# GpSimd's share of a depthwise convolution: the tap as a tensor operand, and five of six sums made by accumulating DMAs

## The chip, the cores and the metric

The kernel runs on one core of a Trainium2 chip, as one launch. The metric is device time in microseconds (us), the median of several executions. Beside it there is a profile: one execution recorded by the hardware profiler, with every instruction's start and duration on the five engines: TensorE (PE in the profile; its weight loads are PEld), VectorE (DVE), ScalarE (ACT), GpSimd (POOL) and SyncE (SP), and with the DMA engines' work. A "q" behind an engine's name is its queue of DMA issues and semaphore waits.

## The reference

A causal depthwise convolution along the sequence (7 taps, softmax-normalised, one set for each of 8 heads of 24 channels), followed by a gated feed-forward network whose last two matrices are multiplied with nothing between them.

```python
# x: (8, 3904, 192), weight: (8, 7)
w = exp(weight - max) / (sum + 1e-09)              # over the 7 taps
x_pad = concatenate([zeros(B, 6, D), x], axis=1)   # each of the 8 sequences begins with zeros
out = einsum('hk,bskhg->bshg', w, x_unf)           # out[s] = sum over k of w[h,k] * x_pad[s+k]
...
a = x @ w1            # x: (31232, 192), w1, w2: (192, 1024)
b = x @ w2
h = a * b @ w3        # w3: (1024, 1024)
return h @ w_out      # w_out: (1024, 192)
```

Inputs and output are fp32; the kernel multiplies in bf16.

## The kernel before, in words

**Rounds and phases.** The 31232 tokens are taken as two streams of 15616 (`NS = 2`), each in rounds of `CH = 512` tokens: 31 rounds, both streams together in a round. `w3 @ w_out` is formed once at the start (`W_sb`), so that a round has two parts on TensorE. In `first_product(R)` (L599) eight tiles of 128 columns of `x @ w1` and `x @ w2` go to PSUM (`pa`, `pb`); ScalarE copies `pa` to `asb` (L606) and VectorE multiplies `asb` by `pb` into `abT` (L608). In `second_product(R, r)` (L624) `abT @ W_sb` is formed for one stream; ScalarE copies the result to `osb` (L629) and SP's queue stores it (L638). Three rounds make a phase: three first products, then the six second products of the three rounds, then the next phase. `abT` has three buffers, one for each round of a phase.

**The convolution, in three ways.** The first products need the convolved `x` transposed: channels on partitions (64 of each stream), tokens along the free dimension, three groups `k` of 64 channels. Most rounds get it from TensorE: GpSimd loads windows of `x` into `xb` (L158), a small matmul with banded weights convolves them (`conv`, L331, at the places between second products that the table `places` lists), the result goes to DRAM as `rows` and comes back through DMA transposes into a ring, `xT` (L429). Where a sequence begins inside a window, GpSimd clears rows of `xb` (`clear`, L863) before `conv` reads them. The rounds of the phases named in `SIDE` get theirs another way, as "side tasks": GpSimd casts `x` to bf16 in DRAM (`rows_c`, L483), a DMA transpose on SP's queue brings a piece with 16 tokens of halo to SBUF as `raw` (L492), and a sum over seven shifted products gives a part of `side`: ScalarE makes the first product (`side_first`), VectorE the other six as one instruction each (`side_sums`, L515). VectorE's sums run during the second products, from a plan that is worked out beforehand.

**GpSimd's half tasks.** Seven halves of such tasks (512 tokens, channel group 2) are GpSimd's: `BY_POOL`, one in each phase from the third phase of the kernel on. SP's queue brings the raw piece by one transpose (L536, `pool_transpose`) at the end of a phase's first products. In the next phase `pool_sums` gives seven jobs: the first (d = 1) writes tap times shifted raw to `acc` in fp32; the next five (d = 2 to 6) write the product to `tmp` (L542) and add `tmp` to `acc` (L562); the last (d = 0) writes a product to `tmp` and adds it to `acc` into `side` in bf16 (L557). `tmp` is one tile of 128 x 512 fp32.

**What sets GpSimd's order.** GpSimd runs its list in order. Each phase from the second on has eight pacing points inside its first products (`points`). At each, a tiny copy from the `abT` tile just written (`pace`, L879) makes GpSimd wait until VectorE has come so far; then come the `xb` loads or `rows_c` casts that are due at this point, issued from GpSimd's own DMA queue, and then one job of the half task. At the seventh point of a phase that has convolutions, `clear` stands ahead of the cast and the job. A DMA issue that must wait for something waits in the engine's queue, with everything behind it.

Of the kernel before, what the change touches and what calls it, by code (L numbers as in the profile page):

```python
# [8 lines left out]
FP32 = mybir.dt.float32  # L9
BF16 = mybir.dt.bfloat16  # L10
AX = mybir.AxisListType
ALU = mybir.AluOpType
# [4 lines left out]
def kernel(  # L17
# [10 lines left out]
    nc = tc.nc  # L28

    B, S, D = x.shape  # L30
    H, K = weight.shape
# [7 lines left out]
    CH = 512  # L39
# [30 lines left out]
    t0 = (LAG + 3) * CH  # L70
# [19 lines left out]
    const = ctx.enter_context(tc.tile_pool(name="const", bufs=1))  # L90
# [90 lines left out]
    for r in range(NS):  # L181
# [13 lines left out]
        out=diag, in_=diag, pattern=[[-1, 128 + 8]], compare_op=ALU.is_equal,  # L195
# [13 lines left out]
    for i in range(4):  # L209
        d = diag[i * C:i * C + C, i * C + 2 * i:i * C + 2 * i + C]  # L210
        nc.vector.tensor_copy(
            out=cmask[i * C:i * C + C],
            in_=bass.AP(tensor=d.tensor, offset=d.offset, ap=[d.ap[0], [1, 2], [1, C]]))
# [45 lines left out]
    for i in range(3):  # L259
# [3 lines left out]
        out=share[:, :, 0:K], in0=taps.unsqueeze(1).to_broadcast([H, H, K]), scalar=total,  # L263
        in1=diag[0:H, 0:H].unsqueeze(2).to_broadcast([H, H, K]), op0=ALU.mult, op1=ALU.mult)
    spread = banks("spread")
    for i in range(4):
# [6 lines left out]
        out=wsb, in_=spread[:, 0, 0:2 * H].rearrange("p (h k) -> p h k", h=H)  # L273
# [5 lines left out]
        out=cprod.rearrange("p h k (s two) -> p h k s two", two=2),  # L279
        in0=cmask.rearrange("p k (s two) -> p k s two", two=2).unsqueeze(1)  # L280
            .to_broadcast([128, H, 2, C // 2, 2]),
        in1=wsb.unsqueeze(3).to_broadcast([128, H, 2, C // 2, 2]),
        op=ALU.mult)
# [6 lines left out]
    for k in range(2):  # L290
# [5 lines left out]
                          in_=bps[:, 0, 0:C * H].rearrange("p (h s) -> p h s", s=C))  # L296
# [137 lines left out]
    wC = const.tile([128, NP, K], FP32)  # L434
# [85 lines left out]
        size = (t1 - t0) / (2 * CH)  # L520
        return [(size, job(d, d == 0)) for d in list(range(2, K)) + [0]]

    pool_raw, pool_acc, pool_tmp = [], [], const.tile([128, CH], FP32, name="tmp")

    def pool_tiles():
        t = stage.tile([128, 3 * CH + HALO], BF16, tag="wo", bufs=1, name="acc")
# [3 lines left out]
    def pool_half(p, k, half):  # L530
        lo = half_of(p, half)[0]
        return p, k, lo, [z for z in range(0, TS, S) if lo <= z < lo + CH]
# [5 lines left out]
    def pool_sums(p, k, half):  # L538
        _, _, t0, starts = pool_half(p, k, half)

        def product(out, d):
            nc.gpsimd.tensor_scalar(  # L542
                out=out, in0=pool_raw[0][:, HALO - d:HALO - d + CH],
                scalar1=wC[:, k, K - 1 - d:K - d], scalar2=None, op0=ALU.mult)

        def job(d):
            def run():
                acc, tmp = pool_acc[0], pool_tmp
                if d == 1:
                    product(acc, 1)  # L550
                    for z in starts:
                        nc.gpsimd.memset(acc[:, z - t0:z - t0 + 1], 0.0)
                    return
                product(tmp, d)
                if d == 0:
                    o = half * CH
                    nc.gpsimd.tensor_tensor(out=side_of[p][:, k, o:o + CH], in0=acc, in1=tmp,  # L557
                                            op=ALU.add)
                    return
                for lo, hi in zip([t0] + [z + d for z in starts], starts + [t0 + CH]):  # L560
                    a = acc[:, lo - t0:hi - t0]
                    nc.gpsimd.tensor_tensor(out=a, in0=a, in1=tmp[:, lo - t0:hi - t0],  # L562
                                            op=ALU.add)
            return run
        return [job(d) for d in list(range(1, K)) + [0]]

# [382 lines left out]
```

## Time and profile before

| | us |
|---|---|
| median of 3 runs (lowest, highest) | 512.19 (511.61, 513.01) |
| span of the profiled execution, first to last instruction | 509.2 |
| TensorE busy | 504.4 |
| VectorE busy | 446.6 |
| ScalarE busy | 347.4 |
| GpSimd busy | 229.3 |

The page names no other time of the profiled execution than its span; the run's time is some 3 us above it. The granted TensorE clock is 1.000 over the span. Rows of a group give line, engine, operation, output and inputs, shapes, the count, then the busy time in us, the mean duration in ns and the idle time just before. Rows of a timeline give start and duration in us, then line, engine, operation and count. Rows of DMA issues end with the size in KB and the median time in us from issue to landing. A row of waits gives the waiting engine, tile and line, what released it, then the total in us, the number of times and the longest.

### The profile page before, as it was taken

The page shows a single profiled execution, that of the slowest core. Times are in us where ns is not written, and L with a number is a line of the kernel's source. Part 1 is how long each engine was busy: PE and PEld are TensorE (multiplying, and loading weights), DVE is VectorE, ACT ScalarE, POOL GpSimd, SP SyncE. Part 2 cuts the span into 40 slices and gives each one's busy share as a digit, 9 for nine tenths or more (in the row PEclk, how much of TensorE's full clock was granted, in tenths as well). Part 3 has the DMA queues.
Part 4 walks back from the last instruction along what each step waited for, and adds up shares of the span by engine and source line. Part 5 has one row for each costly group of instructions (what it writes and reads, how often), then busy time and mean ns, then how long its engine had stood idle before and what let it go on. Part 6 is the DMA issues. An engine that isn't in the chain of part 4 may idle for free.

```text
span 509.2 us, 13689 instructions
## 1 busy us (share of the span) xinstructions
PE 504.4 (99%) x5761; PEld 338.9 (67%) x5761; DVE 446.6 (88%) x403; ACT 347.4 (68%) x387; POOL 229.3 (45%) x303
## 2 busy tenths in 40 slices
PE   8999999999999999999999999999999999999997
PEld 4546865595569557855875596569557855965597
DVE  7898769999999799899989999999899999999930
ACT  6786667836778776477667767763776477457752
POOL 9966101333990597079519902970573067100000
PEclk9999999999999999999999999999999999999999
DMA  9999979999966999973889337986501500230025
GB/s 135 161 158 179 171 145 181 149 158 190 166 60 160 142 158 126 237 79 23 65 220 95 25 105 123 194 111 158 102 0 44 156 2 0 84 106 1 1 64 156
DMA packets 156825, 58.45 MB, mean 115 GB/s; under 512 B 112607, under 2 KB 156763, under 8 KB 156763
## 3 DMA queue, kind: packets, MB, share of 16 engines
q1 hardware_dynamic: 86043, 40.62, 38.0%
q0 software_dynamic: 70560, 16.85, 37.2%
q8 instruction: 45, 0.74, 0.6%
q14 instruction: 17, 0.14, 0.1%
q10 hardware_dynamic: 160, 0.10, 0.1%
HBM read 33.97 MB, written 34.85 MB: 135 GB/s over the span
## 4 chain that ended last, share of the span: by engine, by line
PE 98%; DVE 1%; ACT 0%; issue 0%
PE ops L624 32%; PE pa L599 31%; PE pb L599 31%; PE cps L331 1%; PE wps L696 1%; PE warm L241 1%; PE tps L404 0%; PE ops L649 0%; PE tps L419 0%; DVE abT L608 0%; PE cps L360 0%; ACT asb L606 0%; ACT convo L340 0%; DVE xb L285 0%; DVE Aband L295 0%
## 5 line engine op out<-in xcount | busy, mean ns | idle before, releaser
L608 DVE TENSOR_TENSOR abT<-asb,pb 128x1024 bf16<-128x1024 bf16 x240 | 292.7, 1221 | 30.4 <-ACT asb L606 14.5
L606 ACT CAST asb<-pa 128x1024 bf16<-128x1024 f32 x244 | 247.0, 1012 | 64.2 <-PE pa L599 64.0
L599 PEld LDWEIGHTS <-wn 64*128 64x128 bf16 x1488 | 138.5, 94 | 79.7 <-issue 1.6
L599 PEld LDWEIGHTS <-ws 64*128 64x128 bf16 x1488 | 129.7, 94 | 70.0 <-issue 1.4
L624 PE MATMUL ops<-W_sb,abT 128*128 128x192 bf16 x1936 | 163.7, 246 | 0.0
L624 PEld LDWEIGHTS <-abT 128*128 128x128 bf16 x1936 | 158.5, 98 | 6.4 <-issue 6.4
L599 PE MATMUL pb<-xT,wn 64*128 64x512 bf16 x408 | 111.2, 376 | 0.0
L599 PE MATMUL pa<-xT,wn 64*128 64x512 bf16 x408 | 110.1, 376 | 0.1
L599 PE MATMUL pa<-xT,ws 64*128 64x512 bf16 x408 | 110.2, 376 | 0.0
L599 PE MATMUL pb<-xT,ws 64*128 64x512 bf16 x408 | 108.5, 376 | 0.0
L629 ACT COPY osb<-ops 128x768 f32<-128x768 f32 (+1 forms) x61 | 48.5, 795 | 84.7 <-PE ops L624 82.8
L879 POOL COPY pace<-abT 1x2 bf16<-1x2 bf16 x57 | 10.9, 192 | 175.2 <-DVE abT L608 175.2
L599 PE MATMUL pb<-side,wn 64*128 64x512 bf16 (+1 forms) x336 | 88.8, 368 | 0.0
L599 PE MATMUL pa<-side,wn 64*128 64x512 bf16 (+1 forms) x336 | 87.3, 369 | 0.0
L599 PE MATMUL pa<-side,ws 64*128 64x512 bf16 (+1 forms) x336 | 87.3, 369 | 0.0
L515 DVE SCALAR_TENSOR_TENSOR acc<-raw,wC,acc 128x1024 f32<-128x1024 bf16 (+2 forms) x70 | 84.8, 1212 | 2.0
L599 PE MATMUL pb<-side,ws 64*128 64x512 bf16 (+1 forms) x336 | 85.7, 368 | 0.0
L542 POOL TENSOR_SCALAR tmp<-acc,wC 128x512 f32<-128x512 bf16 x42 | 65.7, 1565 | 1.2
L562 POOL TENSOR_TENSOR acc<-acc,tmp 128x512 f32<-128x512 f32 x35 | 44.4, 1268 | 2.9
L483 POOL DMA_DIRECT2D rows_c<-in_x_dram x50 | 37.1, 745 | 4.9 <-issue 2.8
L158 POOL DMA_DIRECT2D xb<-in_x_dram x50 | 32.3, 650 | 7.5 <-DMA xb<-in_x_dram 2.1
L515 DVE SCALAR_TENSOR_TENSOR acc<-side,wC,acc 128x1024 f32<-128x1024 bf16 (+1 forms) x20 | 24.3, 1217 | 3.8 <-DMA rows<-convo 3.2
(78 smaller groups left out, 188.5 us busy)
## 6 DMA issues: line engine op xcount, KB each, us to landing
out_dram<-osb SPq DMA_DIRECT2D x54, 384.0 KB
xb<-in_x_dram POOLq DMA_DIRECT2D x16, 240.0 KB, 7.6
out_dram<-osb SPq DMA_DIRECT2D x12, 192.0 KB
rows_c<-in_x_dram POOLq DMA_DIRECT2D x16, 130.0 KB, 4.6
rows_c<-in_x_dram POOLq DMA_DIRECT2D x12, 128.0 KB, 5.7
rows<-convo SPq DMA_DIRECT2D x6, 240.0 KB
xb<-in_x_dram POOLq DMA_DIRECT2D x6, 228.0 KB, 4.5
w3b<-in_moe_w_dram POOLq DMA_DIRECT2D x4, 256.0 KB, 5.4
```

The source lines that it names most:

```text
L158: nc.gpsimd.dma_start(out=tiles[js[0]][0][group(r, e), s:s + w, :], in_=bass.AP(tensor=x.tensor, offset=(r * TS + t - PAD) * D, ap=[[D, C] ...
L241: nc.tensor.matmul(t[:, j % 2, 0:wd].rearrange("p (a c) -> p a c", c=128), zeros, zeros.unsqueeze(1).to_broadcast([128, wd // 128, 128]), ...
L483: nc.gpsimd.dma_start(out=rows_c[lo:t1, k, r * Q:r * Q + Q], in_=x_rows[r * TS + lo:r * TS + t1, k * Q:k * Q + Q])
L515: nc.vector.scalar_tensor_tensor(out=side_of[p][:, k, o:o + t1 - t0] if last else a, in0=raw[:, HALO + lo - t0 - d:HALO + hi - t0 - d], sc ...
L542: nc.gpsimd.tensor_scalar(out=out, in0=pool_raw[0][:, HALO - d:HALO - d + CH], scalar1=wC[:, k, K - 1 - d:K - d], scalar2=None, op0=ALU.mult)
L562: nc.gpsimd.tensor_tensor(out=a, in0=a, in1=tmp[:, lo - t0:hi - t0], op=ALU.add)
L599: nc.tensor.matmul(p[:, r, f * N:f * N + N], w_of(i, k, r)[rs, ft * 128:(ft + 1) * 128], operand(R, k, rs), start=(k == 0), stop=(k == NP ...
L606: nc.scalar.copy(out=asb[:, :, 0:per * N], in_=pa[:, :, 0:per * N])
L608: nc.vector.tensor_tensor(out=ab[:, f0, :, 0:N], in0=asb[:, :, 0:N], in1=pb[:, :, 0:N], op=ALU.mult)
L624: nc.tensor.matmul(ops[:, g // 2, (g % 2) * D:(g % 2) * D + D], ab[:, jt, r, g * 128:(g + 1) * 128], W_sb[:, jt, :], start=(jt == 0), stop ...
L629: nc.scalar.copy(out=osb.rearrange("p (a g) d -> p a (g d)", g=2), in_=ops[:, 0:ng // 2, 0:2 * D])
L879: P(out=pace, in_=abT_of[R][0:1, ft, 1, 0:2])
```

## The change

`tmp` becomes two tiles that alternate with the tap. The product is a `tensor_tensor` whose second operand is the tap broadcast along the free dimension (step 0) in place of a `tensor_scalar` with the tap as a scalar. The sums of d = 2 to 6 are DMAs from GpSimd's queue that add `tmp` into `acc` in SBUF, in fp32; the last sum (d = 0) stays an instruction of GpSimd. In all seven tasks none of the five sums is split by a sequence's beginning, so there are 35 such DMAs of 128 x 512. On TensorE, VectorE and ScalarE the instructions and their order are as before, and so is the order of GpSimd's list, with the new instructions in the place of the old. Each accumulating DMA waits for the one before it on `acc` and for the product in `tmp`; the product of d = 0 waits for the DMA of d = 6, which reads the same `tmp`.

```diff
-    pool_raw, pool_acc, pool_tmp = [], [], const.tile([128, CH], FP32, name="tmp")
+    pool_raw, pool_acc = [], []
+    pool_tmp = [const.tile([128, CH], FP32, name=f"tmp{v}", tag=f"tmp{v}") for v in range(2)]
...
         def product(out, d):
-            nc.gpsimd.tensor_scalar(
+            nc.gpsimd.tensor_tensor(
                 out=out, in0=pool_raw[0][:, HALO - d:HALO - d + CH],
-                scalar1=wC[:, k, K - 1 - d:K - d], scalar2=None, op0=ALU.mult)
+                in1=wC[:, k, K - 1 - d:K - d].to_broadcast([128, CH]), op=ALU.mult)
 
         def job(d):
             def run():
-                acc, tmp = pool_acc[0], pool_tmp
+                acc, tmp = pool_acc[0], pool_tmp[d % 2]
...
                 for lo, hi in zip([t0] + [z + d for z in starts], starts + [t0 + CH]):
-                    a = acc[:, lo - t0:hi - t0]
-                    nc.gpsimd.tensor_tensor(out=a, in0=a, in1=tmp[:, lo - t0:hi - t0],
-                                            op=ALU.add)
+                    nc.gpsimd.dma_start(out=acc[:, lo - t0:hi - t0],
+                                        in_=tmp[:, lo - t0:hi - t0], accum_op=ALU.add)
```

## The prediction

> **What bounds the kernel now.** I read the page's busy times first, then the chain that ended last, then who waited on TensorE.
>
> ```profile
> span 509.2 us, 13689 instructions
> PE 504.4 (99%) x5761; PEld 338.9 (67%) x5761; DVE 446.6 (88%) x403; ACT 347.4 (68%) x387; POOL 229.3 (45%) x303
> PE 98%; DVE 1%; ACT 0%; issue 0%
> PE warm L241 <- DVE zeros L180: 1.1, 1, 1.1
> PE cps L331 <- DVE Aband L295: 0.3, 1, 0.3
> PE tps L419 <- ACT convo L340: 0.2, 1, 0.2
> L542 POOL TENSOR_SCALAR tmp<-acc,wC 128x512 f32<-128x512 bf16 x42 | 65.7, 1565 | 1.2
> L562 POOL TENSOR_TENSOR acc<-acc,tmp 128x512 f32<-128x512 f32 x35 | 44.4, 1268 | 2.9
> ```
>
> TensorE is busy 504.4 of 509.2 us and carries 98% of the chain; all its waits for others add up to 1.6 us, at the start (lines four to six). GpSimd (POOL) is not on the chain, so nothing taken off it shortens the run by itself. It can only lengthen it, by being late for TensorE. So I looked for where GpSimd's results meet TensorE with the least time in between. That is the end of the first products of the phase that begins at 117 us, the first with a half task:
>
> ```profile
> 126.02 0.17 POOL L879 COPY pace<-abT 1x2 bf16<-1x2 bf16 x1
> 126.14 1.36 POOL L158 DMA_DIRECT2D xb<-in_x_dram  x2
> 127.53 1.57 POOL L542 TENSOR_SCALAR tmp<-acc,wC 128x512 f32<-128x512 bf16 x1
> 129.19 1.27 POOL L562 TENSOR_TENSOR acc<-acc,tmp 128x512 f32<-128x512 f32 x1
> 130.40 0.18 POOL L879 COPY pace<-abT 1x2 bf16<-1x2 bf16 x1
> 130.52 0.85 POOL L483 DMA_DIRECT2D rows_c<-in_x_dram  x1
> 131.41 1.57 POOL L542 TENSOR_SCALAR tmp<-acc,wC 128x512 f32<-128x512 bf16 x1
> ...
> 145.92 0.18 POOL L879 COPY pace<-abT 1x2 bf16<-1x2 bf16 x1
> 146.15 0.56 POOL L863 MEMSET xb<- 6x192 bf16 x2
> ...
> 149.06 1.27 POOL L557 TENSOR_TENSOR side<-acc,tmp 128x512 bf16<-128x512 f32 x1
> 150.28 1.17 POOL L879 COPY pace<-abT 1x2 bf16<-1x2 bf16 x1
> ```
> ```profile
> 148.20 2.81 PE L624 MATMUL ops<-W_sb,abT 128*128 128x192 bf16 x32
> 150.94 0.42 PE L331 MATMUL cps<-xb,Aband 32*32 32x240 bf16 x30
> ```
> ```profile
> L331 PEldq EVENT_SEMAPHORE  x5: 51/51/51, 5.0 to 150.3; - x5
> ```
>
> One round at a pacing point costs GpSimd 3.9 us (130.40 to 134.3: pace copy, cast, product, sum). The two memsets (L863) clear rows of `xb` that the convolution at 150.94 reads; the last row shows TensorE's semaphore for it, at 150.3. The memsets end at 146.15 + 0.56 = 146.71, so this meeting has 150.94 - 146.71 = 4.2 us to spare, the least of any. TensorE is in order: a memset later than that stops it.
>
> **The change part by part.** *The product* (49 times L542) takes its tap as a second tensor. No row has this form; bounds are 1.27 us (L562, two tensors) and 1.57 us (as now). By form the first is nearer: I take 1.27. It saves 49 x 0.3 = 15 us of GpSimd, worth nothing on the chain.
>
> *The sums.* 35 x 1.27 = 44.4 us of GpSimd go; 35 DMA issues come, at about 0.60 us by the next-named row (35 x 0.60 = 21 us), each of 256 KB, added into `acc`.
>
> ```profile
> L677 POOL DMA_DIRECT2D w3b<-in_moe_w_dram x12 | 7.1, 599 | 1.3 <-DMA xb<-in_x_dram 1.3
> ```
>
> On GpSimd's own time the change is a gain. But *each accumulating DMA waits until the one before it on `acc` has landed*, and the wait stands in GpSimd's queue: behind it stand the next pace copy, the next cast or `xb` load, the next product and, in this phase, the memsets. Sum d issued at T is followed by pace, cast and product (0.17 + 0.85 + 1.27, some 3 us with the issue), then GpSimd stands until T + L, L being the time from issue to landing. The chain's step is max(3.0, L), against 3.9 now. No row shows an accumulating DMA; the nearest are
>
> ```profile
> rows_c<-in_x_dram POOLq DMA_DIRECT2D x4, 130.0 KB, 4.0
> xb<-in_x_dram POOLq DMA_DIRECT2D x2, 216.0 KB, 7.9
> rows_c<-in_x_dram POOLq DMA_DIRECT2D x2, 64.0 KB, 2.6
> ```
> ```profile
> xb<-in_x_dram POOLq DMA_DIRECT2D x6, 228.0 KB, 4.5
> w3b<-in_moe_w_dram POOLq DMA_DIRECT2D x4, 256.0 KB, 5.4
> DMA  9999979999966999973889337986501500230025
> ```
> ```profile
> DMA  6447999999699999999900699209900694001670
> ```
>
> the first three and the last (slices of 0.875 us) from the DMA view of 120 to 155 us alone. Below 2.6 there is no reason to go, above 7.9 (two loads behind each other on saturated engines) neither. `w3b` reads 512 KB in fp32 and writes 256 KB, the same bytes as an accumulate (two fp32 operands read, one written): 5.4, in a burst. A sum has one 130 KB cast for company in each step instead of a burst; its row is 4.0. I take L = 5.0, nearer to the row with the same bytes. Cheaper than that, by the first: 4.0.
>
> By the Trainium skill, DMA: Bandwidth & Descriptors, section Anatomy of one DMA — SWDGE (gpsimd) path, a DMA from this queue costs about 2.0 us plus its bytes at 436 GB/s, as an estimate 2.6 us here, or 3.2 with the read doubled. By it no wait would be left and the time would be the present one, while the trace's loaded rows (4.0 to 7.9) lie above it; it stands beside the second rival below.
>
> *The sum for this phase.* The first product ends at 127.53 + 1.27, so the first accumulate is issued at 128.9. It lies behind two `xb` loads (126.14, 7.9 us: landing at 134.0 and, issued 0.7 later, 134.7), in a stretch where the slices read 9 until 137. For its own transfer behind them I allow the 1.4 us by which the 130 KB cast is longer than the 64 KB one (4.0 - 2.6): it lands at 136.1. The next three sums land at 136.1 + 3L = 151.1; then the sixth sum may be issued (0.6), then pace (0.17, and see below), then both memsets (0.2 + 0.56). Pace now falls beside VectorE's side sums, where it took 1.17 instead of 0.17 (150.28 above, with VectorE's row from 149.84 below): +1.0.
>
> 151.1 + 0.6 + 0.17 + 1.0 + 0.2 + 0.56 = 153.6, against 150.94: TensorE stands 2.7 us, 2.8 with its semaphore (0.05). In general the stall is 3L - 12.2, and nothing from L = 4.1 down: 4.0 us at 5.4, 11.5 at 7.9.
>
> ```profile
> 149.84 6.85 DVE L515 SCALAR_TENSOR_TENSOR acc<-raw,wC,acc 128x1024 f32<-128x1024 bf16 x5
> ...
> 157.93 6.56 DVE L515 SCALAR_TENSOR_TENSOR acc<-raw,wC,acc 128x1024 f32<-128x1024 bf16 x5
> ...
> 167.95 5.05 DVE L608 TENSOR_TENSOR abT<-asb,pb 128x1024 bf16<-128x1024 bf16 x4 [2.14 <-ACT asb L606]
> ```
>
> *VectorE beside a late GpSimd.* The five sums that start at 149.84, beside GpSimd's last add, take 6.85 us, the same five later 6.56. GpSimd's last product and add now fall wholly among such rows; VectorE may lose up to 2 x 1.27 us. Cover: the 2.14 us for which it waits at 167.95, and TensorE's own stall; I cost it at nothing, and at up to 2 us a phase where that cover is gone. The Trainium skill, SBUF — State Buffer, section Who interferes with whom, says that a VectorE instruction with two SBUF inputs contends with a GpSimd instruction that reads SBUF, and that the later one blocks entirely; the 1.17 against 0.17 agrees.
>
> *Later half tasks.* These have no memset to meet; TensorE meets `side` itself, a phase later.
>
> ```profile
> 178.11 1.27 POOL L562 TENSOR_TENSOR acc<-acc,tmp 128x512 f32<-128x512 f32 x1
> ...
> 196.77 1.27 POOL L557 TENSOR_TENSOR side<-acc,tmp 128x512 bf16<-128x512 f32 x1
> ```
> ```profile
> 213.12 0.39 PE L599 MATMUL pa<-side,wn 64*128 64x512 bf16 x1
> ```
>
> In the second one the first sum goes out at 177.7; five landings and the last product and add give 177.7 + 5L + 2.8 = 205.5 at L = 5, for `side` at 213.1: 7.6 us to spare, gone at L = 6.5. The first, third, fifth and sixth tasks have most of a phase or more; the fourth and the seventh are as the second. So one phase pays.
>
> *SP's queue.* The transpose for the next half task (L536) waits for GpSimd's last product, six output stores behind it:
>
> ```profile
> SPq L536 <- POOL tmp L542: 35.6, 2, 20.3
> SPq L395 <- DVE convo L236: 25.7, 1, 25.7
> ```
>
> It stood up to 20.3 us already without TensorE waiting, so 5 to 9 us more cost nothing; if that cover failed, the next phase's half task would begin late by as much.
>
> *Sum.* The span 509.2 + 2.8 = 512.0; what lies around the span is 512.19 (median) - 509.2 = 3.0. Time: 515.0 us.
>
> **The rivals.**
>
> *No wait left: not slower (512.2).* If L is 4.1 or less, as the `rows_c` rows say (2.6, 4.0), the steps fit the pacing and the memsets come by 151 at the latest. For it: SBUF at both ends, and 2 KB per row where a cast moves 128-byte pieces. Against: every row above with 200 KB or more is at 4.5 or above, and the DMA engines read 9 when the first sum goes out. This is also where the Trainium skill's sum above would end.
>
> *The accumulate is dear (525 and up).* At L = 7 the first phase loses 3 x 7 - 12.2 = 8.8 us, and the second half task gives 177.7 + 35 + 2.8 = 215.5 against 213.1: 2.4 more, and the fourth about as much: some 13 us, 525. At 7.9 the first loses 11.5, the second 177.7 + 39.5 + 2.8 - 213.1 = 6.9, the fourth and the seventh up to that: about 540. For it: the `xb` row, and that an add in flight has no price here. Against: those loads stood in line for each other. It decides above L = 6.5.
>
> *Faster.* 44.4 us of sums and the products' 15 leave GpSimd, and VectorE could gain where they shared. Against: TensorE's waits are 1.6 us, none of them on GpSimd; the 0.3 us at 149.84 is the only overlap that I found. At best 511.9.
>
> **How the numbers follow.** Less than 0.3% (1.5 us) counts as no change; a measurement of this kernel can tell about that much. Forecast (L from 4.1 to 6.5, 512.5 to 520): 0.50. No wait left: 0.27. Dear: 0.19. Faster: 0.04. Of the forecast the piece under 1.5 us (L below 4.5) has 0.05, so same is 0.32, slower 0.64, faster 0.04. The predicted time is the forecast's 515.0. For 8 in 10 the range takes in the second rival from 511.7 and the dear one to L = 7.3, 530; left out are the faster case, scatter below 511.7, and the dear case's upper half. The forecast's own range is 512.5 to 520.
>
> **What would show it.** The issue-to-landing time of the new `acc<-tmp` DMAs: 5 us is right, under 4 is the second rival, over 6.5 the third. GpSimd's waits: DMA issues on L562 held by the DMA before, about 2 us each, 4 to a task. TensorE's waits: one on the memset of L863 near 151 us, of 3 us, and none elsewhere; the phases after it unchanged in length. The products: 1.27 us. The prediction is wrong if TensorE shows no wait on GpSimd, or shows waits on `side`, or if VectorE's wait of 2.14 us at a phase's start vanishes and TensorE waits there instead.

## The result, and the profile after

| | before | after |
|---|---|---|
| median (lowest to highest), us | 512.3 (511.61 to 513.01) | 515.58 (514.04 to 517.42) |
| ratio to before, 95% interval | | 1.0082 (1.0063 to 1.0101) |
| span of the profiled execution, us | 509.2 | 515.6 |

The kernel is slower. The interval, taken on 512.3, is 3.2 to 5.2 us. The four executions do not lie around one value: 514.04 and 514.43 had a granted TensorE clock of 1.000 over the span (spans 512.3 and 512.7), 516.73 and 517.42 one of 0.997 (spans 514.9 and 515.6). The profile that follows is of the one at 517.42. In every execution on record whose span was noted the time is 1.6 to 1.9 us above the span. The 3.0 us that stood around the span of before are thus some 1.8, and the other 1.2 us, as an estimate, are what the profiled execution was quicker than the median.

The page, with the engines' busy times, the chain that ended last and the waits of TensorE, answers to the first fence of the prediction; among them stand GpSimd's products and the new DMAs (median us to landing):

```profile
span 515.6 us, 13720 instructions
PE 506.7 (98%) x5761; PEld 340.3 (66%) x5761; DVE 453.4 (88%) x403; ACT 347.5 (67%) x387; POOL 199.6 (39%) x303
PE 84%; DVE 4%; issue 4%; POOL 3%; DMA 3%; SPq 1%; ACT 1%; POOLq 0%; DVEq 0%
L543 POOL TENSOR_TENSOR tmp<-acc,wC 128x512 f32<-128x512 bf16 x42 | 51.5, 1225 | 15.9 <-DMA acc<-tmp 15.8
acc<-tmp POOLq DMA_DIRECT2D x35, 256.0 KB, 3.8
PE cps L331 <- POOL xb L863: 2.5, 1, 2.5
PE pb L599 <- DVE abT L608: 1.4, 2, 0.8
```

GpSimd's busy time fell from 229.3 to 199.6 us, and the run became longer. TensorE's share of the chain fell from 98% to 84%, and DMA, GpSimd and "issue" (the wait of a DMA issue for the landing before it is booked partly as that) came into it. TensorE has waits that it did not have: one on the memsets of L863, and two small ones on VectorE's `abT`.

GpSimd's timeline of the first half task (start, duration, line, operation; idle time ahead in brackets) answers to the rows from 126.02 to 146.15 of before:

```profile
128.78 0.96 POOL L562 DMA_DIRECT2D acc<-tmp  x1 [0.31 <-POOL tmp L543]
...
138.23 0.90 POOL L562 DMA_DIRECT2D acc<-tmp  x1 [6.56 <-issue]
...
143.76 0.89 POOL L562 DMA_DIRECT2D acc<-tmp  x1 [2.70 <-issue]
...
148.56 0.90 POOL L562 DMA_DIRECT2D acc<-tmp  x1 [2.00 <-issue]
...
150.11 2.04 POOL L543 TENSOR_TENSOR tmp<-acc,wC 128x512 f32<-128x512 bf16 x1
152.56 0.90 POOL L562 DMA_DIRECT2D acc<-tmp  x1 [0.41 <-POOL tmp L543]
153.18 0.32 POOL L879 COPY pace<-abT 1x2 bf16<-1x2 bf16 x1
153.54 0.56 POOL L863 MEMSET xb<- 6x192 bf16 x2
```

From one accumulate to the next it takes 9.45, 5.53, 4.80 and 4.00 us, where one round took 3.9 before. The brackets show GpSimd standing for 6.56, 2.70 and 2.00 us ahead of a DMA. The profile names no releaser for these three; by the time to landing of the DMA before (8.9, 4.7 and 4.2 us in the DMA view of each), every one of them ended 0.6 to 0.8 us after that landing. The memsets, at 146.15 before, come at 153.54. TensorE's timeline at that place:

```profile
148.32 2.81 PE L624 MATMUL ops<-W_sb,abT 128*128 128x192 bf16 x32
151.07 0.30 PE L331 MATMUL cps<-xb,Aband 32*32 32x240 bf16 x10
153.84 0.69 PE L331 MATMUL cps<-xb,Aband 32*32 32x240 bf16 x22 [2.48 <-POOL xb L863]
154.47 4.36 PE L624 MATMUL ops<-W_sb,abT 128*128 128x192 bf16 x32
158.76 0.45 PE L331 MATMUL cps<-xb,Aband 32*32 32x240 bf16 x32
```

The wait is in the third row, 2.48 us. The rows around it are longer too: the convolution, now in two parts, takes 0.30 + 0.69 us for the 0.42 of one block, and the 32 matmuls behind it 4.36 us where such 32 take 2.81 in the first row. That is 0.57 + 1.55 us on top of the wait. The table of stretches of the same execution has the reason for the 1.55 (length, busy time of each engine with its count, granted clock, DMA share, GB/s):

```profile
152.00:156.00 4.00, 2.11 (x38) 1.74 (x38) 3.89 (x4) 1.40 (x2) 2.20 (x6) 0.94 0.98 114
156.00:160.00 4.00, 4.00 (x61) 3.31 (x60) 3.14 (x2) 1.55 (x4) 3.55 (x2) 0.64 0.96 67
160.00:164.00 4.00, 4.00 (x51) 4.00 (x50) 1.37 (x2) 3.25 (x5) 1.02 (x3) 1.00 0.28 20
```

The clock was 0.94 in the stretch with the wait, 0.64 in the next, and 1.00 after it. These are means: in stretches of half a microsecond the clock is 1.00 up to 155.5 us, 0.50 from there to 158.9, and 1.00 again. So TensorE ran at half speed for 3.4 us, and that began 1.7 us after it had resumed at 153.84. By the Trainium skill, TensorE: Matmul & The Clock Gate, Part 1, the clock halves after an idle window of about 3.4 us; the trace agrees on the half, but here it fell behind a wait of 2.5 us, so the measurement puts the point lower.

The rest lies later, ahead of two phases that begin at 314 and at 362 us, and comes through VectorE. For the first of them, VectorE's timeline, then GpSimd's, then TensorE's rows that waited:

```profile
300.01 8.11 DVE L515 SCALAR_TENSOR_TENSOR acc<-raw,wC,acc 128x1024 f32<-128x1024 bf16 x5
```
```profile
303.48 1.35 POOL L543 TENSOR_TENSOR tmp<-acc,wC 128x512 f32<-128x512 bf16 x1 [2.15 <-DMA acc<-tmp]
304.91 2.13 POOL L558 TENSOR_TENSOR side<-acc,tmp 128x512 bf16<-128x512 f32 x1
```
```profile
318.30 0.37 PE L599 MATMUL pb<-side,wn 64*128 64x512 bf16 x1 [0.85 <-DVE abT L608]
...
366.18 0.37 PE L599 MATMUL pb<-xT,wn 64*128 64x512 bf16 x1 [0.57 <-DVE abT L608]
```

Five sums that took 6.56 us before take 8.11, while GpSimd's last product and add stand among them, held back by landings. VectorE then reaches the next first products late, and TensorE waits 0.85 us for `abT`; the same again a phase later, 0.57.

Where the time went, from the lengths of TensorE's phases in the two profiles: the second products of the phase from 117 us 22.42 against 17.78 (+4.64: 2.48 wait, 0.57 for the split convolution, 1.55 for the clock), the first products from 314 us +0.97, those from 362 us +0.69, and +0.1 near the start. That is 6.4 us = 515.6 - 509.2. The two executions with clock 1.000 have spans 3.1 and 3.5 us above 509.2, less than 6.4 - 1.55; how the 3.1 to 3.5 split up there no profile shows.

### The profile page after: what moved, and what is told of

Same layout as the page of the kernel before. It is cut to its first block, busy times and chain, and to the rows that moved or that the text cites. A ratio compares the mean times of both kernels' runs of the same rounds, so it can differ in the third digit from the quotient of the medians.

```text
span 515.6 us, 13720 instructions
## 1 busy us (share of the span) xinstructions
PE 506.7 (98%) x5761; PEld 340.3 (66%) x5761; DVE 453.4 (88%) x403; ACT 347.5 (67%) x387; POOL 199.6 (39%) x303
## 4 chain that ended last, share of the span: by engine, by line
PE 84%; DVE 4%; issue 4%; POOL 3%; DMA 3%; SPq 1%; ACT 1%; POOLq 0%; DVEq 0%
PE ops L624 28%; PE pa L599 27%; PE pb L599 27%; DVE acc L515 3%; DMA acc<-tmp 1%; DVE abT L608 1%; PE cps L331 1%; SPq L492 1%; PE wps L696 1%; DMA wn<-in_moe_w_dram 1%; POOL tmp L543 1%; ACT asb L606 1%; POOL xb L158 1%; DMA acc<-rows_c 0%; PE tps L404 0%
## 5 line engine op out<-in xcount | busy, mean ns | idle before, releaser
L515 DVE SCALAR_TENSOR_TENSOR acc<-raw,wC,acc 128x1024 f32<-128x1024 bf16 (+2 forms) x70 | 90.1, 1287 | 5.4 <-ACT acc L497 3.4
L879 POOL COPY pace<-abT 1x2 bf16<-1x2 bf16 x57 | 16.4, 287 | 138.8 <-DVE abT L608 138.7
L543 POOL TENSOR_TENSOR tmp<-acc,wC 128x512 f32<-128x512 bf16 x42 | 51.5, 1225 | 15.9 <-DMA acc<-tmp 15.8
L562 POOL DMA_DIRECT2D acc<-tmp x35 | 31.6, 902 | 62.3 <-issue 32.5
L483 POOL DMA_DIRECT2D rows_c<-in_x_dram x50 | 39.3, 790 | 3.2 <-issue 3.1
L340 ACT CAST convo<-cps 128x320 bf16<-128x320 f32 (+4 forms) x42 | 25.0, 670 | 4.2 <-PE cps L331 4.2
```

What stands on the lines that cost most here:

```text
L340: f(out=convo[:, e::E, k, :, lo:lo + c] .rearrange("p w r g -> p r w g"), in_=src[:, :, :, o:o + c])
L483: nc.gpsimd.dma_start(out=rows_c[lo:t1, k, r * Q:r * Q + Q], in_=x_rows[r * TS + lo:r * TS + t1, k * Q:k * Q + Q])
L515: nc.vector.scalar_tensor_tensor(out=side_of[p][:, k, o:o + t1 - t0] if last else a, in0=raw[:, HALO + lo - t0 - d:HALO + hi - t0 - d], sc ...
L543: nc.gpsimd.tensor_tensor(out=out, in0=pool_raw[0][:, HALO - d:HALO - d + CH], in1=wC[:, k, K - 1 - d:K - d].to_broadcast([128, CH]), op=A ...
L562: nc.gpsimd.dma_start(out=acc[:, lo - t0:hi - t0], in_=tmp[:, lo - t0:hi - t0], accum_op=ALU.add)
L879: P(out=pace, in_=abT_of[R][0:1, ft, 1, 0:2])
```

## The experiments

Theory: the chain of landings holds back the memsets of L863, and TensorE's wait there, with what it brings along, is the loss. Rivals: the 35 transfers load the DMA engines for everyone; the new product disturbs VectorE; or GpSimd's lateness as such costs VectorE time, wherever it comes from. The third column counts the executions whose mean granted clock over the span was below 0.9985.

| experiment | median (range), us | executions with less clock | ratio to before (95%) |
|---|---|---|---|
| e1, memsets ahead of the chain | 515.21 (512.94 to 518.46) | 4 of 12 | 1.0075 (1.0051 to 1.0100) |
| e2, the product alone | 511.05 (510.84 to 512.18) | 0 of 11 | 0.9991 (0.9975 to 1.0006) |
| e3, DMAs in the first task alone | 514.38 (512.23 to 516.78) | 3 of 10 | 1.0054 (1.0030 to 1.0077) |
| e4, DMAs in all tasks but the first | 513.17 (512.63 to 516.20) | 3 of 12 | 1.0044 (1.0023 to 1.0065) |
| e5, two accumulators | 513.05 (511.96 to 514.27) | 0 of 7 | 1.0037 (1.0023 to 1.0050) |
| e6, kernel before, memsets held by 8 us | 516.97 (515.24 to 519.05) | 5 of 6 | 1.0113 (1.0092 to 1.0134) |
| e7, kernel before with 35 unread DMAs | 512.57 (511.96 to 515.81) | 3 of 10 | 1.0039 (1.0022 to 1.0056) |
| e8, copying DMAs | 511.65 (one execution) | | |
| e9, DMAs in the fourth and fifth task | 512.78 (511.98 to 513.89) | 0 of 8 | 1.0030 (1.0020 to 1.0040) |
| e10, as e7 with the new product | 510.95 (510.84 to 512.06) | 1 of 11 | 0.9995 (0.9986 to 1.0004) |
| e11, as e6, held by 5.8 us | 512.88 (512.45 to 513.48) | 0 of 6 | 1.0029 (1.0018 to 1.0041) |

The kernel before, on the same chips, had medians of 511.05 to 511.21.

### e1: the memsets at the fifth pacing point of that phase, in place of the seventh

```diff
         if p in places:
-            at[last - 1].insert(0, clear)
+            at[4 if p == 2 else last - 1].insert(0, clear)
```

> The changed kernel with one move: in the phase from 117 us the memsets of xb stand at the fifth pacing point instead of the seventh. Theory (late memset): TensorE's wait on L863 (2.5 us) and the lower granted clock behind it go; what is left is VectorE's lateness at the start of two later phases, up to 1.4 us: 512.3 to 514.0 us. Rival (the 9 MB that the accumulating DMAs move slow the other transfers): nothing changes, 515 to 516.

The wait on L863 is gone, as expected. The time did not follow: 515.21, above the 512.3 to 514 that was expected and within the 515 to 516 of the rival, the load (e10, below, speaks against that one). TensorE's waits and GpSimd's timeline of e1:

```profile
PE pb L599 <- DVE abT L608: 2.2, 2, 1.5
PE pa L599 <- POOL side L558: 1.5, 1, 1.5
```
```profile
177.67 0.93 POOL L562 DMA_DIRECT2D acc<-tmp  x1 [0.31 <-POOL tmp L543]
...
210.84 2.06 POOL L543 TENSOR_TENSOR tmp<-acc,wC 128x512 f32<-128x512 bf16 x1 [6.11 <-DMA acc<-tmp]
212.97 2.12 POOL L558 TENSOR_TENSOR side<-acc,tmp 128x512 bf16<-128x512 f32 x1
```

The same DMA in the profile of the change:

```profile
182.53 0.93 POOL L562 DMA_DIRECT2D acc<-tmp  x1 [0.31 <-POOL tmp L543]
```

In e1 the second half task runs up to the time when TensorE needs `side`. Its first accumulate goes out at 177.67, its last product starts at 210.84, 33.2 us later, and `side` is done at 215.09; TensorE was there at about 213.6. In the change the same stretch took 27.5 us (182.53 to 210.05), and `side` was done in time.

It is tempting to say that the change's stall in the first phase had paid for this second meeting. The two profiles speak against it. GpSimd is tied to TensorE by the pacing copies, so the stall moved both: the first accumulate goes out 4.86 us earlier in e1, and TensorE begins the phase in which it needs `side` 4.86 us earlier too (213.01 for 217.87). In both there are 35.3 us from the one to the other. What differs is how long the landings took, and why they took longer in e1's profiled execution no run shows.

TensorE's phases in e1 say where its 4.1 us of span are: the first products from 213 us are 1.71 longer than before (the wait on `side`), those from 311 us 1.67 and those from 360 us 0.82 (the waits on `abT`). So taking away the one wait that a profile shows gave back nothing that can be measured, because other meetings, with landings that differ from profile to profile, cost as much.

### e2: the product alone

```diff
-            nc.gpsimd.tensor_scalar(
+            nc.gpsimd.tensor_tensor(
                 out=out, in0=pool_raw[0][:, HALO - d:HALO - d + CH],
-                scalar1=wC[:, k, K - 1 - d:K - d], scalar2=None, op0=ALU.mult)
+                in1=wC[:, k, K - 1 - d:K - d].to_broadcast([128, CH]), op=ALU.mult)
```

> The kernel before with the product as tensor_tensor and the five sums left on GpSimd. Theory: GpSimd is ahead of its old times by some 0.4 us a step, TensorE waits for nothing: 512.2 +- 0.6 us, no change. Rival (a two-operand product contends with VectorE, or is itself dear): 513 or more, and VectorE's L515 or L608 rows longer than before.

Level with before. The page of e2 and its groups show what the form costs by itself:

```profile
PE 504.0 (99%) x5761; PEld 338.9 (67%) x5761; DVE 445.7 (88%) x403; ACT 347.4 (68%) x387; POOL 204.2 (40%) x303
L542 POOL TENSOR_TENSOR tmp<-acc,wC 128x512 f32<-128x512 bf16 x42 | 43.8, 1044 | 0.5
```

1.04 us for 1.57: 25 us less for GpSimd, which is on nobody's path. Half of the change is free of harm and of use; the loss is in the DMAs.

### e3 and e4: the DMAs in the first half task alone, and in all but the first

```diff
+                    a = acc[:, lo - t0:hi - t0]
+                    if (p, half) == (5, 0):
+                        nc.gpsimd.dma_start(out=a, in_=tmp[:, lo - t0:hi - t0],
+                                            accum_op=ALU.add)
+                    else:
+                        nc.gpsimd.tensor_tensor(out=a, in0=a, in1=tmp[:, lo - t0:hi - t0],
+                                                op=ALU.add)
```

e4 has `!=` in place of `==`.

> The changed kernel with accumulating DMAs in the first half task alone (5 of the 35); the other six sum on GpSimd. Theory: the whole of the memset's wait is here, 2.5 us and the clock behind it, and the waits on VectorE at later phases are gone: 514.2 to 516.5 us. Rival (DMA load): a seventh of the loss, 512.7.

> The changed kernel with accumulating DMAs in six half tasks, the first one summing on GpSimd as before. Theory: no wait on L863, clock 1.00 throughout; only VectorE's lateness of up to 1.4 us: 512.3 to 514.0 us. Rival (DMA load): six sevenths of the loss, 515.

e3 is 1.0054: with five of the 35 DMAs, most of the loss. Its wait and the stretch behind it:

```profile
PE cps L331 <- POOL xb L868: 2.7, 1, 2.7
```
```profile
156.00:160.00 4.00, 4.00 (x61) 3.54 (x60) 3.93 (x3) 1.45 (x3) 3.79 (x3) 0.67 0.69 54
```

The same wait, the same fall of the clock behind it, and no wait of TensorE for `abT`. e4 has no wait on the memsets, three waits on VectorE's `abT` of 1.7 us in all, and is 1.0044. Its profiled execution has no stretch of lower clock, as expected, but three of its twelve executions had less clock. The two ratios less one add up to 0.0098, the change has 0.0082 (0.0063 to 0.0101): two losses, one in each part, that can be told apart. e4 also bears on e1: it has no stall in the first phase either, its second task took 29.2 us from the first accumulate to the last product (178.16 to 207.34), against 33.2 in e1 and 27.5 in the change, and only e1's came too late for `side`.

### e5: even taps to a second accumulator

```diff
+    acc_b = const.tile([128, CH], FP32, name="acc_b", tag="acc_b")
...
-                acc, tmp = pool_acc[0], pool_tmp[d % 2]
+                acc, tmp = (pool_acc[0], acc_b)[d % 2 == 0], pool_tmp[d % 2]
...
+                if d == 2:
+                    product(acc, 2)
...
+                if d == 0:
+                    nc.gpsimd.tensor_tensor(out=tmp, in0=acc, in1=tmp, op=ALU.add)
+                    acc = pool_acc[0]
```

Four DMAs to a task are left, and each waits for the one two back. (`cprod`, a tile of the start, shares its place with another to make room.)

> The changed kernel with two accumulators: odd taps go to acc, even taps to a second tile, and GpSimd adds the two at the end. Each task has 4 accumulating DMAs instead of 5, and each waits for the one two before it instead of the last. Theory (the chain of landings makes GpSimd late): GpSimd's waits on L562's DMAs fall to a fraction, TensorE waits neither on the memset nor on side, and GpSimd ends before VectorE's side sums: within 0.2% of the kernel before. Rival (DMA load: four fifths of the bytes remain): ratio 1.005 to 1.008.

The waits in GpSimd's queue went as the theory says, all but the one ahead of the last product, and so did the wait on the memsets:

```profile
POOL tmp L544 <- DMA acc_b<-tmp: 14.6, 7, 5.1
...
PE pb L607 <- DVE abT L616: 0.6, 2, 0.4
```

By the ratios (1.0037 and 1.0082) the kernel is some 2 us faster than the change and, against the expectation, still 1.9 us slower than before. The profile accounts for less: the two first products behind late sums are 0.45 and 0.50 us longer, and the profiled execution, at 512.17, was among the quicker. Where the rest lies in the others is open.

### e6 and e11: the kernel before, with the memsets held back by other work

```diff
+    idle = const.tile([128, CH], FP32, name="idle")
+    def hold():
+        for _ in range(14):
+            nc.gpsimd.memset(idle, 0.0)
...
+            if p == 2:
+                at[last - 1].insert(0, hold)
```

e11 has 10 in place of 14.

> The kernel before, with no accumulating DMA; in the phase from 117 us GpSimd writes 14 times a spare tile of 128x512 (some 0.45 us each, 6.3 us, an estimate) ahead of the two memsets of xb. Theory: TensorE waits for L863 as it does in the changed kernel, 6.3 - 4.2 = 2 us if a write takes 0.45, the run is longer by that, and in some executions by up to 2 us more with the granted clock below 1.00 behind the wait: 512.5 to 516 us. Rival (the DMAs are the cause): no change.

> The kernel with 14 writes of a spare tile ahead of the memsets, with 10 instead (0.54 us each in the trace of the 14): TensorE's wait on L863 should be 5.4 - 4.2 = 1.2 us. If the granted clock falls behind any wait of that length, the run is longer by up to 3 us and most executions show a clock under 1.00; if a short wait leaves the clock alone, the run is longer by 1.2 us, ratio 1.002 to 1.003.

No DMA is added. GpSimd's timeline of e6, TensorE's wait, and the stretch behind it:

```profile
146.17 8.08 POOL L870 MEMSET idle<- 128x512 f32 x14
154.30 0.56 POOL L863 MEMSET xb<- 6x192 bf16 x2
```
```profile
PE cps L331 <- POOL xb L863: 3.3, 1, 3.3
```
```profile
156.00:160.00 4.00, 4.00 (x61) 3.45 (x60) 2.03 (x2) 1.45 (x3) 3.90 (x4) 0.65 0.29 20
```

e6 makes the first loss of the change with the kernel before, and a larger one: the wait is 3.3 us, the clock falls to 0.65 behind it, and the phase's second products are 5.55 us longer (23.33 against 17.78). Five of its six executions had less clock. The median, 516.97, is above the 512.5 to 516 that was expected; the 14 writes took 8.08 us where 6.3 were assumed. TensorE's timeline of e11 and one of its stretches:

```profile
151.16 0.30 PE L331 MATMUL cps<-xb,Aband 32*32 32x240 bf16 x10
152.18 0.69 PE L331 MATMUL cps<-xb,Aband 32*32 32x240 bf16 x22 [0.71 <-POOL xb L863]
152.81 2.81 PE L624 MATMUL ops<-W_sb,abT 128*128 128x192 bf16 x32
```
```profile
156.00:160.00 4.00, 4.00 (x50) 4.00 (x50) 3.76 (x3) 4.00 (x7) 2.53 (x3) 1.00 0.25 16
```

With memsets 2.4 us earlier the wait is 0.71 (1.2 was expected), the clock stays at 1.00, and the 32 matmuls take 2.81 as before. The convolution is 0.30 + 0.69 here too, so those 0.57 us come from its being split and not from the clock; 0.71 + 0.57 is the 1.29 us by which this stretch is longer. The lateness of the memsets is enough for the loss without a DMA, and a stop at this place costs its wait and some 0.6 us. The stops of 2.5, 2.7 and 3.3 us that were profiled (the change, e3, e6) were each followed by 3.4 us at half the clock, those of up to 1.5 us (e11's 0.7 and both of e1's) were not. What decides it is not shown: executions with less clock also came up in e1, e4 and e7, whose profiles have no wait on the memsets, and in 4 of the 69 executions of the kernel before that were run beside the experiments.

### e7 and e10: the transfers without the chain

```diff
+                nc.gpsimd.dma_start(out=spare[d % 2], in_=wn[0].bitcast(FP32), accum_op=ALU.add)
```

The line stands behind each of the 35 sums, which stay instructions of GpSimd; nothing reads `spare`. In both kernels the memsets go to the fourth point of their phase. e10 has the new product besides.

> The kernel before with all its sums on GpSimd, and beside each of the 35 sums one accumulating DMA of the same 256 KB from a weight tile into one of two spare tiles that nothing reads (the output is as before); the memsets of xb stand at the fourth pacing point, so that GpSimd's longer steps do not meet TensorE there. Theory: the load alone does little; GpSimd is some 0.9 us a step later; within 0.3% of the kernel before. Rival (DMA load): ratio 1.005 or more, with the same transfers late.

> The kernel with the load of 35 unread accumulating DMAs once more, with the product as tensor_tensor (1.05 us where it took 1.57 to 1.79), so that GpSimd ends its tasks some 3 us earlier with the same DMAs in flight. Theory (port): VectorE's side sums in the phase that begins near 261 us are held up less, 6.6 to 7.0 us for the five that took 7.59; TensorE's waits on VectorE fall under 0.4 us in all; ratio 1.000 to 1.002. Rival (DMA load): as with the slow product, 1.004.

e7 by itself seemed to speak for the load: 1.0039, above the 0.3% that was expected and below the 1.005 of the rival. Its profile says something else. GpSimd does the old product, the sum and the issue (0.9 us) in each round, so it ends late, and VectorE's five sums beside it are longer. GpSimd's and VectorE's timelines of e7:

```profile
293.84 1.77 POOL L546 TENSOR_SCALAR tmp<-acc,wC 128x512 f32<-128x512 bf16 x1
295.69 1.27 POOL L561 TENSOR_TENSOR side<-acc,tmp 128x512 bf16<-128x512 f32 x1
```
```profile
295.73 7.59 DVE L515 SCALAR_TENSOR_TENSOR acc<-raw,wC,acc 128x1024 f32<-128x1024 bf16 x5
```

and e10's DMA issues and the same two timelines, where the product is short and GpSimd is done before VectorE begins:

```profile
spare<-wn POOLq DMA_DIRECT2D x35, 256.0 KB, 3.8
```
```profile
292.33 1.27 POOL L561 TENSOR_TENSOR side<-acc,tmp 128x512 bf16<-128x512 f32 x1
```
```profile
295.58 6.56 DVE L515 SCALAR_TENSOR_TENSOR acc<-raw,wC,acc 128x1024 f32<-128x1024 bf16 x5
```

e10 issues the same 35 accumulates with the same landing time, and is level with before. That settles two rivals at once: these transfers as a load, outside the chain, cost nothing that can be measured, and what hurts VectorE is GpSimd's product and add among its sums, whatever made them late.

### e8: copies in place of accumulates

```diff
                     nc.gpsimd.dma_start(out=acc[:, lo - t0:hi - t0],
-                                        in_=tmp[:, lo - t0:hi - t0], accum_op=ALU.add)
+                                        in_=tmp[:, lo - t0:hi - t0])
```

> The changed kernel with its 35 DMAs copying tmp onto acc instead of adding (the five middle sums are left out of the result). The waits stand as they are. Theory: the landing is mostly fixed time and queueing, so it falls from 3.8 us by under 1 us in the median, and TensorE still waits for the memset, 1 to 2.5 us. Rival (the add is what is dear): landing near 2.5 us and no wait on L863.

The DMAs and GpSimd's timeline of e8:

```profile
acc<-tmp POOLq DMA_DIRECT2D x35, 256.0 KB, 2.8
```
```profile
147.68 0.56 POOL L863 MEMSET xb<- 6x192 bf16 x2
```

The addition costs 1.0 us of landing time (3.8 against 2.8). Without it the chain keeps pace well enough: the memsets end at 148.24, ahead of the convolution at 151, and TensorE does not wait for them; the wait that was expected here did not come, and the rival (landing near 2.5 us, no wait on L863) was nearer. There is one execution, at 511.65.

### e9: DMAs in the fourth and fifth half task alone

```diff
-                    if (p, half) == (5, 0):
+                    if (p, half) in ((8, 1), (12, 0)):
```

(The line is that of e3.)

> The changed kernel with accumulating DMAs in the fourth and fifth half tasks alone (10 of the 35), those whose phases ended with TensorE waiting for VectorE. Theory (GpSimd's late product and add hold VectorE's side sums up, through the SBUF port that they share): both waits of TensorE on VectorE are there, 0.6 to 1.6 us each, and the loss is that of the kernel with six such tasks, ratio 1.003 to 1.005. Rival (DMA load): ten of thirty DMAs, a third of that loss, 1.0015.

1.0030: these two tasks alone cost 1.6 us on the median. VectorE's row and TensorE's wait in e9:

```profile
296.34 8.23 DVE L515 SCALAR_TENSOR_TENSOR acc<-raw,wC,acc 128x1024 f32<-128x1024 bf16 x5
```
```profile
PE pb L604 <- DVE abT L613: 1.6, 2, 1.0
```

The sums are 1.67 us longer than 6.56, and the two first products that follow 1.1 and 0.8 us longer. This is the loss of e4 in its own place.

## Why the prediction was right, and what it left out

**Direction and mechanism: right, and shown.** GpSimd was off the path and could only lengthen the run by being late; the meeting with the least slack was the memsets of L863; the chain of landings made them late. e3 has the wait with the first task alone, e6 has it with no DMA at all, e4 and e1 lose it when that one lateness goes. 515.0 was forecast, 515.58 is the median. That the two are so close is in part luck. The sum takes 3.0 us for what lies around the span, and the executions on record have 1.8; with that, the span 509.2 and the stall 2.8 it would have been 513.8. The loss in the profiled execution was 6.4 us of span, larger than the 2.8 of the sum, by two terms that were left out of it, below.

**The terms of the first phase.**

| term | forecast | profile after |
|---|---|---|
| first landing | 136.1 | 137.7 (issue at 128.78, landing 8.9 later); the next issue starts at 138.2 |
| step of the chain, three times | 5.0, 15.0 in all | 5.53, 4.80, 4.00, 14.3 in all |
| issue on GpSimd | 0.6 | 0.90 |
| pace copy | 1.17 | 0.32 |
| product | 1.27 | 1.03 to 2.05, mean 1.23 |
| memsets done | 153.6 | 154.1 |
| TensorE's wait | 2.8 | 2.5 |

The forecast's L was a time to landing; the median over all 35 is 3.8, 4.2 in the window of this phase (8.9, 4.7, 4.2, 3.4, 3.7), and a step is that and 0.6 to 0.8 us until the next issue starts. So the step was sized right and its parts were not: landing shorter, issue and product longer. The first accumulate took 8.9 us where the sum, with 1.4 us for standing behind both `xb` loads, had 7.2 (128.9 to 136.1); whether the loads made all of it no run shows. The 1.0 us for the pace copy did not come (0.32): a product beside VectorE's sums took the delay in its place (2.04 us at 150.11), and it was this product, not a landing, that released the last accumulate.

**"One wait on the memset, and none elsewhere": the second half was wrong.** The prediction named the lateness of GpSimd beside VectorE's sums, priced it at up to 2 us a phase where cover is gone, and then costed it at nothing. In the fourth and fifth task the cover was gone: 0.97 and 0.69 us, TensorE waiting for `abT`. e9 shows it alone and e10 shows it vanish when GpSimd ends in time. This is the last of the prediction's own signs of being wrong, VectorE's wait at the start of a phase gone and TensorE waiting there instead, at two phases other than the one that it named; at that one VectorE still waits 2.22 us in the profile after. What should have been asked of the profile before is VectorE's wait at the start of *each* phase; the one quoted had 2.14 us, these two have 0.49 and 0.77 (VectorE's timeline of before):

```profile
311.31 3.76 DVE L608 TENSOR_TENSOR abT<-asb,pb 128x1024 bf16<-128x1024 bf16 x3 [0.49 <-ACT asb L606]
...
358.50 3.75 DVE L608 TENSOR_TENSOR abT<-asb,pb 128x1024 bf16<-128x1024 bf16 x3 [0.77 <-ACT asb L606]
```

A lengthening of 8.11 - 6.56 = 1.55 us less a cover of 0.49 is 1.06, and TensorE's stretch grew by 0.97; less 0.77 it is 0.78, against 0.69 (the second phase's sums are longer by the same 1.55: 5.90 + 2.17 us for 5.24 + 1.28). The cover could be read from the profile of before, and the price, up to 2 us, was there. The Trainium skill, SBUF — State Buffer, section Who interferes with whom, describes the cause (VectorE with two SBUF inputs against a reading GpSimd); the 1.55 us, and the 2.04 and 2.13 us of GpSimd's product and add where 1.04 and 1.27 are their times alone, agree with it.

**The clock behind the wait: not in the sum.** A stop of TensorE was costed at its own length. In the profiled execution 0.57 us for the split convolution and 1.55 us of slower matmuls came on top of 2.48. The second is a term of its own that does not always come: two of the change's four executions had less clock, and five of six of e6's, but none of e11's, where the wait was 0.71 us. One stretch of 3.4 us at half speed lowers the mean over some 512 us by 0.003, an estimate, and 0.997 is what the change's two show. Why some executions of one kernel have it and others not, and what stopped TensorE in those of e1, e4 and e7 that had it, wasn't settled.

**Later tasks.** The formula 177.7 + 5L + 2.8 with its limit at L = 6.5 was the right one: in e1 the five steps took 33.2 us, 6.6 each, and `side` came at 215.1, against 213.5 by the formula; the rest is the product and add, 4.2 us beside VectorE in place of 2.8. In the change itself the five steps took 27.5 us, 5.5 each, and `side` was done at 213.3 for a phase that began at 217.9. The stall does not explain that margin of 4.6 us: the first accumulate had gone out later by as much as TensorE had (e1, above). So "one phase pays" held for the `side` meetings in the change because L stayed under the limit, and in e1's profiled execution it did not.

**The rivals.** *No wait left* was tied to L under 4.1. The median landing is 3.8, and yet the wait came: a step of the chain is more than a landing (14.3 us for three, in a loaded phase), and the first landing alone was 1.6 us later than allowed for, 2.1 by the issue behind it. *Dear* needed 6.5 and more in the change itself; in e1 the second task was at its limit, 6.6. *Faster* had nothing to gain: e2 takes 25 us from GpSimd and measures 0.9991 (0.9975 to 1.0006).

No version tried here is faster than the kernel before; TensorE was busy for 504.4 of 509.2 us.

## What to carry to other kernels

Moving work from an engine's instructions to a chain of DMAs trades its busy time for landing times, and a chain in an in-order queue delays everything behind it: find the result of that engine which its consumer needs with least slack, and cost the chain up to there with landings from a loaded stretch. On a kernel bound by one engine, less work on another was worth nothing here (e2), and lateness cost in three places: the wait itself, the clock behind it, and the instructions of a neighbour among which the late work falls (6.56 us became 8.11). Don't expect back what a profile books to one wait: with that wait gone e1 lost as much at other meetings, since the landings there were longer. And before calling that a stall which had paid for the others, check whether it had moved the supplier along with the consumer, as it had here.

## What the runs showed of the hardware that was not expected

- After waits of TensorE of 2.5, 2.7 and 3.3 us (the change, e3, e6) the granted clock was 0.50 for 3.4 us, from 0.8 to 1.7 us after TensorE had resumed; as the mean of a stretch of 4 us it shows as 0.64 to 0.67. After waits of 0.7 us (e11) and 1.5 us (e1) it stayed at 1.00.
- An accumulating DMA of 256 KB in fp32 within SBUF landed after 3.8 us (3.2 to 8.9) where a plain copy took 2.8, and its issue held GpSimd for 0.90 us instead of 0.61.
- GpSimd's product of 128 x 512 by a tap of step 0 took 1.04 us alone, that with a scalar operand 1.57.
